# Attention and feed-forward in one kernel: scores of sequences 1 to 7 with queries on partitions, exponentials turned by DMA transposes

## The chip, the cores and the metric

The kernel runs on one core of one Trainium2 chip. The metric is the device time of one execution, in microseconds (us). The core has five engines, each with its own queue of instructions that it works off strictly in order: TensorE (PE; its weight loads are listed apart as PEld), VectorE (DVE), ScalarE (ACT), GpSimd (POOL) and SyncE (SP, which here issues all DMAs). They wait for one another through semaphores.

## The reference, cut to what matters

Eight sequences of 576 tokens, eight heads of 64. Causal softmax attention is mixed, by a gate per head, with a read from a memory matrix; the result goes through a two-layer feed-forward network (FFN).

```python
scores = q @ k.T / sqrt(64)                      # per sequence and head, 576 x 576
scores = where(causal, -1e9, scores)
a = exp(scores - scores.max(-1)); a /= a.sum(-1) + 1e-9
local = a @ v
mem_out = (phi(q) @ M_prev) / (phi(q) @ z_prev + 1e-6)
x = g * mem_out + (1 - g) * local                # 4608 tokens x 512
h = x @ w_in                                     # 512 -> 2048
out = (h * clip(h + 3, 0, 6) / 6) @ w_out        # 2048 -> 512
```

## The kernel before

**FFN.** 4608 tokens are 18 blocks of 256. A block has 8 pieces of the first product (`ffn1`, L510: 24 matmuls of 256 columns into a PSUM tile `ph`, of which there are two; then ACT, DVE, ACT and DVE at L531 to L534 make the two float16 parts of `g`) and 8 pieces of the second (`ffn2`, L536: 12 matmuls of 512 columns; after four pieces ACT moves the sum out at L554 and SP stores it). Float32 products are made of three float16 products, high by high, high by low and low by high. Block 0 and the whole of sequence 0 use float32 matmuls instead.

**Attention.** A unit is one head of one sequence with one group of 128-query blocks: blocks 0 and 1 together, block 2, block 3, block 4 (64 queries). With 8 heads that is 32 units a sequence. Of sequences 1 to 7 a unit goes through these steps:

- `scores` (L330): keys on partitions, queries along the row. For each tile of 128 keys two matmuls (L347, L348: high and low part of q) and, for the tile on the diagonal, a third one that adds the causal mask (L350).
- `reduce` (L352): the maximum over the key tiles on DVE (L360; block 0 is copied by ACT, L358), and then over partitions by POOL's `partition_all_reduce` (L362).
- `sub` (L364): DVE takes the maximum off (L368). `exp` (L375): ACT makes the exponentials (L377), and POOL writes them as float16, `ah`, with an `affine_select` whose condition always holds (L381).
- `lo` (L384): DVE makes the low part, `al` (L389).
- `pv` (L391): with `ah` and `al` as weights, three matmuls a key tile against v (L413 to L415), and two against the memory (L417).
- `combine` (L419): DVE and ACT divide, scale and add (L430 to L438).

**Preparation.** While a sequence is worked on, the four pairs of heads of the next are loaded and split into float16 parts (`prep_steps`, L162). Each pair has one `partition_all_reduce` on POOL (L186) for its scales, whose result DVE takes up at L190 and L143; each sequence's memory has one (L298), and each FFN block one for the scale of its x (L472). SP moves the halves of q, k and phi(q) into stacked tiles (L210, L211, L218) and turns x with `dma_start_transpose` (L496).

**Order.** The loop at L731 emits unit t's scores, unit t-1's exponentials and unit t-2's products, with FFN pieces between. `at` (L135) gives everything emitted a priority in pieces of the FFN; a scheduler then puts each engine's instructions into one fixed order. Five of the FFN's 18 blocks are left to the end (`TAIL`, L50).

Of the kernel before, what the change touches and what calls it, by code (L numbers as in the profile page):

```python
# [12 lines left out]
F32 = mybir.dt.float32  # L13
# [49 lines left out]
) + PREP_AT[2:]  # L63
LN_SA = float(np.log(SA))


@with_exitstack
def kernel(ctx, tc, qT, kT, v, mz, beta, w_in, w_out, out):
    nc = tc.nc
    PE, DVE, ACT, POOL, SP = nc.tensor, nc.vector, nc.scalar, nc.gpsimd, nc.sync  # L70
    B, NP, _, S = qT.shape          # 8, 4, 128, 576
    H = 2 * NP
    D = 64
    NT, DM = out.shape              # 4608, 512
# [41 lines left out]
    kst, qhl, qps, vst, raw, nat = [], [], [], [], [], []  # L116
    for i in range(NSLOT):
        sizes = [2 * NB * P, 4 * S, 2 * S, NB * 2 * 129]
        whole = const.tile([P, sum(sizes) + 2], F16, name=f"slot{i}")
        at = 0  # L120
        for lst, n, pat, kw in zip((kst, qhl, qps, vst), sizes,
                                   ["p (h s) -> p h s", "p (x h s) -> p x h s", "p (h s) -> p h s",
                                    "p (t h e) -> p t h e"],
                                   [dict(h=2), dict(x=2, h=2), dict(h=2), dict(t=NB, h=2)]):
            lst.append(whole[:, at:at + n].rearrange(pat, **kw))
            at += n
# [33 lines left out]
    slots = {}  # L160

    def prep_steps(b, p):  # L162
# [25 lines left out]
        def scale():  # L188
# [5 lines left out]
            DVE.scalar_tensor_tensor(scal[:, 0:1], i[:, 0:1], 0.125, i[:, 1:2], op0=ALU.mult, op1=ALU.mult)  # L194
            DVE.tensor_scalar(scal[:, 1:2], s[:, 0:1], s[:, 1:2], 8.0 * LN_SA, op0=ALU.mult, op1=ALU.mult)
# [5 lines left out]
            esc, shift = scal[:, 0:1], scal[:, 1:2]  # L201
            slots[b, p] = dict(sl=sl, esc=esc, shift=shift, coef=coef, eps=eps)
# [43 lines left out]
    def nat_load(p, part):  # L246
        """a pair of heads of sequence 0, for float32 products"""
# [65 lines left out]
    # a unit: some 128-query blocks of one head, their scores in one PSUM bank, keys on partitions  # L313
    UNITS = [(0, 1), (2,), (3,), (4,)]
    xtiles = {}
    groups = {}

    class Unit:
        def __init__(self, b, u, p, h):
            self.b, self.u, self.p, self.h = b, u, p, h  # L320
            self.blocks = []
            c = mcol = 0
            for i in UNITS[u]:
                self.blocks.append((i, rows[i], c, mcol))
                c += (i + 1) * rows[i]
# [483 lines left out]
```

## Time and profile before

| | |
|---|---|
| time, two runs | 1120.67 and 1122.51 us, median 1121.59 us |
| span of the profiled execution, first to last instruction | 1120.2 us |
| mean granted TensorE clock | 0.996 |
| HBM read, written | 48.14 MB, 9.44 MB |

The span of the profiled execution and the time of the runs differ by 1.4 us, so what lies outside the span is small. In the profile an engine's busy time is a sum over its instructions; matmuls are pipelined, so a matmul's own duration (0.27 us for 256 columns) is longer than the distance at which the next one starts (0.11 us). What a matmul costs is read from that distance. A group row gives the source line, the engine, the operation, what is written from what, the shape, the count, the busy sum, the mean of one, and the idle time of the engine in front of it with what ended that.

### The profile page before, as it was taken

The page shows a single profiled execution, that of the slowest core. Times are in us where ns is not written, and L with a number is a line of the kernel's source. Part 1 is how long each engine was busy: PE and PEld are TensorE (multiplying, and loading weights), DVE is VectorE, ACT ScalarE, POOL GpSimd, SP SyncE. Part 2 cuts the span into 40 slices and gives each one's busy share as a digit, 9 for nine tenths or more (in the row PEclk, how much of TensorE's full clock was granted, in tenths as well). Part 3 has the DMA queues.
Part 4 walks back from the last instruction along what each step waited for, and adds up shares of the span by engine and source line. Part 5 has one row for each costly group of instructions (what it writes and reads, how often), then busy time and mean ns, then how long its engine had stood idle before and what let it go on. Part 6 is the DMA issues. An engine that isn't in the chain of part 4 may idle for free.

```text
span 1120.2 us, 28768 instructions
## 1 busy us (share of the span) xinstructions
PE 1083.2 (97%) x10736; PEld 797.4 (71%) x10736; DVE 930.7 (83%) x2436; ACT 791.1 (71%) x1880; POOL 412.2 (37%) x544
## 2 busy tenths in 40 slices
PE   8999999999999899999999999999999999999998
PEld 6888767586767667676768576867685868685664
DVE  5999889899899969998999988888799968893321
ACT  5787879677877778787877787668686857563321
POOL 3322223444444433554244533354344433341000
PEclk9999999999999999999999999999999999999999
DMA  8734452333424343315332434233404230101100
GB/s 263 291 100 160 119 135 70 94 91 87 116 84 106 70 118 89 97 45 138 97 76 71 101 96 102 76 92 97 116 22 107 77 69 14 36 5 36 27 13 19
DMA packets 101468, 101.39 MB, mean 91 GB/s; under 512 B 50256, under 2 KB 80976, under 8 KB 101328
## 3 DMA queue, kind: packets, MB, share of 16 engines
q1 hardware_dynamic: 101328, 99.56, 33.1%
q8 instruction: 84, 1.38, 0.5%
q14 instruction: 56, 0.46, 0.1%
HBM read 48.14 MB, written 9.44 MB: 51 GB/s over the span
## 4 chain that ended last, share of the span: by engine, by line
PE 42%; DVE 32%; ACT 8%; issue 8%; DMA 6%; POOL 2%; SPq 1%; DVEq 0%; ACTq 0%; POOLq 0%
DVE a L368 6%; PE po L546 5%; PE po L548 5%; PE po L547 5%; PE ph L523 5%; DVE rm L360 5%; PE ph L524 4%; PE ph L525 4%; DVE al L389 4%; DVE r L532 3%; PE ph L518 3%; DVE g L534 2%; PE sT L343 2%; DVE W L157 2%; POOL mb L362 2%
## 5 line engine op out<-in xcount | busy, mean ns | idle before, releaser
L362 POOL PARTITION_ALL_REDUCE mb<-rm x256 | 251.7, 983 | 336.7 <-DVE rm L360 237.4
L523 PE MATMUL ph<-x,W 128*128 128x256 f16 x1088 | 297.6, 274 | 12.7 <-DVE r L532 7.3
L525 PE MATMUL ph<-x,W 128*128 128x256 f16 x1088 | 297.5, 273 | 0.0
L524 PE MATMUL ph<-x,W 128*128 128x256 f16 x1088 | 297.4, 273 | 0.0
L381 POOL TENSOR_SCALAR_AFFINE_SELECT ah<-a 128x384 f16<-128x384 f32 (+2 forms) x224 | 145.4, 650 | 214.4 <-ACT a L377 105.4
L546 PE MATMUL po<-W,g 128*128 128x512 f16 x544 | 206.6, 380 | 1.9 <-ACT ot L554 1.6
L548 PE MATMUL po<-W,g 128*128 128x512 f16 x544 | 206.5, 380 | 0.8 <-DVE g L534 0.8
L547 PE MATMUL po<-W,g 128*128 128x512 f16 x544 | 206.7, 380 | 0.0
L377 ACT ACTIVATE a<-a,scal 128x384 f32<-128x384 f32 (+2 forms) x224 | 141.6, 633 | 57.0 <-DVE a L368 48.8
L368 DVE SCALAR_TENSOR_TENSOR a<-sT,scal,mb 128x128 f32<-128x128 f32 (+4 forms) x280 | 147.2, 541 | 13.3 <-POOL mb L362 12.4
L360 DVE TENSOR_REDUCE rm<-sT 128x128 f32<-128x256 f32 (+3 forms) x256 | 135.6, 530 | 11.5 <-PE sT L350 4.6
L389 DVE TENSOR_TENSOR al<-a,ah 128x384 f16<-128x384 f32 (+2 forms) x224 | 134.0, 598 | 9.2 <-POOL ah L381 8.0
L532 DVE SCALAR_TENSOR_TENSOR r<-r,ph 128x512 f32<-128x512 f32 x136 | 92.1, 677 | 53.2 <-ACT r L531 52.6
L436 ACT ACTIVATE x<-o,cf 128x64 f32<-128x64 f32 (+1 forms) x320 | 100.6, 314 | 44.2 <-DVE cf L432 39.5
L531 ACT ACTIVATE r<-ph,bias_g,gsc 128x512 f32<-128x512 f32 x136 | 106.5, 783 | 34.2 <-PE ph L525 29.1
L347 PE MATMUL sT<-slot 128*128 128x128 f16 (+1 forms) x840 | 123.7, 210 | 3.9 <-DVE a L368 2.1
L348 PE MATMUL sT<-slot 128*128 128x128 f16 (+1 forms) x840 | 124.3, 210 | 0.0
L523 PEld LDWEIGHTS <-W 128*128 128x128 f16 x1088 | 106.8, 98 | 23.1 <-issue 6.6
L413 PE MATMUL o<-slot,ah 128*128 128x65 f16 (+1 forms) x840 | 116.3, 195 | 6.9 <-ACT y L437 3.6
L533 ACT ACTIVATE g<-r 128x512 f16<-128x512 f32 x136 | 86.4, 636 | 51.2 <-DVE r L532 51.1
L524 PEld LDWEIGHTS <-W 128*128 128x128 f16 x1088 | 106.7, 98 | 19.5 <-issue 5.0
L414 PE MATMUL o<-slot,ah 128*128 128x64 f16 (+1 forms) x840 | 115.4, 195 | 0.0
(149 smaller groups left out, 2387.4 us busy)
## 6 DMA issues: line engine op xcount, KB each, us to landing
slot<-q SPq DMA_DIRECT2D x112, 144.0 KB, 2.5
out<-ot SPq DMA_DIRECT2D x36, 256.0 KB, 2.0
stv<-vn SPq DMA_DIRECT2D x28, 320.0 KB, 3.3
W<-w_in SPq DMA_DIRECT2D x8, 1024.0 KB, 9.5
slot<-w_out SPq DMA_DIRECT2D x8, 1024.0 KB, 4.9
stq<-qT SPq DMA_DIRECT2D x28, 288.0 KB, 3.1
stk<-kT SPq DMA_DIRECT2D x28, 288.0 KB, 3.3
slot<-k SPq DMA_DIRECT2D x112, 72.0 KB, 2.0
```

Of the source, the lines that this page charges most:

```text
L360: DVE.tensor_reduce(rm[:, m0:m0 + nq], src.rearrange("p (t q) -> p q t", q=nq), axis=AX.X, op=ALU.max)
L362: POOL.partition_all_reduce(mb[:, 0:self.m], rm[:, 0:self.m], P, RMAX)
L368: DVE.scalar_tensor_tensor(a[:, c0:c0 + w].rearrange("p (t q) -> p t q", q=nq), self.sT[:, c0:c0 + w].rearrange("p (t q) -> p t q", q=nq), ...
L377: ACT.activation(a, a, AF.Exp, scale=slots[self.b, self.p]["esc"])
L381: POOL.affine_select(self.ah[:, 0:self.n], a, pattern=[[0, self.n]], compare_op=ALU.is_ge, fill=0.0, base=1, channel_multiplier=0)
L389: DVE.tensor_tensor(self.al[:, 0:n], self.a[:, 0:n], self.ah[:, 0:n], op=ALU.subtract)
L523: PE.matmul(ph[:, m], wh, f["xh"][:, c], start=c == 0, stop=False)
L524: PE.matmul(ph[:, m], wh, f["xl"][:, c], start=False, stop=False)
L525: PE.matmul(ph[:, m], wl, f["xh"][:, c], start=False, stop=c == 3)
L546: PE.matmul(po, gh[:, m, ts], W2[:, m, 0:512], start=m == 0, stop=False)
L547: PE.matmul(po, gh[:, m, ts], W2[:, m, 512:], start=False, stop=False)
L548: PE.matmul(po, gl[:, m, ts], W2[:, m, 0:512], start=False, stop=m == 15)
```

## The change

For sequences 1 to 7, and for these alone:

- **Scores** have queries on partitions and keys along the row: for each query block two matmuls (high and low part of k) of up to 512 columns. No mask matmul is left. Block 4 takes both heads of a pair at once, one in partitions 0 to 63 and the other in 64 to 127, in two PSUM tiles (512 and 64 columns), so it has one unit for two heads; a sequence has 28 units.
- **Reduce**: one DVE call (`tensor_tensor_reduce`) scales, adds the mask and keeps the minimum along the row (the scale is negative). POOL's all-reduce of the maximum, DVE's subtraction and ACT's copy are gone.
- **Exp**: ACT with the extremum as bias, one call per query block. POOL then writes the high float16 part with a `tensor_scalar` that multiplies by 256; before, that factor was in the exponent.
- **Lo**: DVE makes the low part. High and low stand side by side in one tile, and SP turns it with one `dma_start_transpose` into tiles with keys on partitions.
- **pv** reads the turned tiles; its matmuls are as many as before. It is emitted three units behind the scores instead of two (`PV_D`).
- q's and k's parts change places in the stacked tiles; a mask is built at the start; `HLB` goes from 3 buffers to 2. The preparation's and the FFN's all-reduces on POOL stay.

```diff
-HLB = 3
+HLB = 2
+AB, A16B, ATB = 2, 2, 2
+PV_D = 3
...
         def do_q():
-            t, hi, lo = pair_tiles("q")
+            _, hi, lo = pair_tiles("q")
             split(hi, lo, st["q"][:, :S], st["s"][:, 0:1])
+            stack(qst[sl], hi, lo)
+
+        def do_k():
+            t, hi, lo = pair_tiles("k")
+            split(hi, lo, st["k"][:, :S], st["s"][:, 1:2])
             for h in range(2):
                 for r in range(2):
-                    SP.dma_start(qhl[sl][D * r:D * r + D, :, h], t[D * h:D * h + D])
...
+                    SP.dma_start(khl[sl][D * r:D * r + D, :, h], t[D * h:D * h + D])
...
-                        kk = kst[sl][:, h, j * P:(j + 1) * P]
-                        PE.matmul(o, kk, qhl[sl][:, 0, h, q0:q0 + nq], start=True, stop=False)
-                        PE.matmul(o, kk, qhl[sl][:, 1, h, q0:q0 + nq], start=False, stop=j < i)
...
+            for i, nq, c0, _ in self.blocks:
+                for h in self.heads:
+                    r0 = D * h if self.both else 0
+                    w = min((i + 1) * P, S)
+                    for part in range(len(self.sT)):
+                        k0, k1 = 512 * part, min(512 * part + 512, w)
+                        o = self.sT[part][r0:r0 + nq, (c0 if part == 0 else 0):][:, 0:k1 - k0]
+                        for x in range(2):
+                            PE.matmul(o, qst[sl][:, h, i * P:i * P + nq], khl[sl][:, x, h, k0:k1],
+                                      start=x == 0, stop=x == 1)
...
+            a = self.a = p2.tile([P, S], F32, name=f"a_{self.id}", tag="a", bufs=AB)
+            nm = self.nm = small.tile([P, 2], F32, name=f"nm_{self.id}", tag="nm", bufs=6)
+            def masked(o, src, m, init, acc):
+                DVE.tensor_tensor_reduce(o, src, m, sd["nesc"], init, ALU.add, ALU.min, acc)
...
-            ACT.activation(a, a, AF.Exp, scale=slots[self.b, self.p]["esc"])
...
-            self.ah = p2.tile([P, 512], F16, name=f"ah_{self.id}", tag="ah")
-            POOL.affine_select(self.ah[:, 0:self.n], a, pattern=[[0, self.n]], compare_op=ALU.is_ge,
-                               fill=0.0, base=1, channel_multiplier=0)
...
+                ACT.activation(a, a, AF.Exp, bias=self.nm[:, c:c + 1], scale=-1.0)
...
+            POOL.tensor_scalar(self.hl[:, 0, 0:self.m], self.a[:, 0:self.m], SA, 1.0, op0=ALU.mult, op1=ALU.mult)
...
-            DVE.tensor_tensor(self.al[:, 0:n], self.a[:, 0:n], self.ah[:, 0:n], op=ALU.subtract)
...
+            DVE.scalar_tensor_tensor(self.hl[:, 1, 0:m], self.a[:, 0:m], SA, self.hl[:, 0, 0:m],
+                                     op0=ALU.mult, op1=ALU.subtract)
+            nb = 2 * self.n // P
+            self.aT = p2.tile([P, 2 * NB, P], F16, name=f"aT_{self.id}", tag="aT", bufs=ATB)
+            SP.dma_start_transpose(out=self.aT[:, 0:nb], in_=self.a16)
```

**What stands where.** On POOL, in the middle of sequence 5 before the change, the all-reduces of the units (`mb`) and the conversions (`ah`) alternate, and the all-reduce of a pair's preparation (`amr`) stands among them:

```order
L381 AFFINE_SELECT ah_2_1_1_9643<-a_2_1_1_9640 128x512
L362 ISA mb_2_2_0_9671<-rm_2_2_0_9670 128x128
L362 ISA mb_2_2_1_9743<-rm_2_2_1_9742 128x128
L381 AFFINE_SELECT ah_2_2_0_9716<-a_2_2_0_9713 128x512
L186 ISA amr_2_10001<-am_2_9994 128x3
L362 ISA mb_2_3_0_9821<-rm_2_3_0_9820 128x128
L381 AFFINE_SELECT ah_2_2_1_9793<-a_2_2_1_9790 128x512
```

and now, at the turn of sequence 3 to 4 (the conversion, L435, is a TENSOR_SCALAR; L190 is the pair's all-reduce, L299 that of the memory):

```order
L190 ISA
L190 ISA amr_3_7427<-am_3_7420 128x3
L435 ISA
L435 TENSOR_SCALAR a_3_3_2_1_7225<-a_3_2_1_7188 128x576
L435 TENSOR_SCALAR a_3_3_3_1_7360<-a_3_3_1_7322 128x576
L435 TENSOR_SCALAR a_4_0_0_0_7442<-a_0_0_0_7403 128x384
L299 ISA
L299 ISA ammr_7501<-amm_7500 128x2
L435 ISA
L435 TENSOR_SCALAR a_4_0_0_1_7509<-a_0_0_1_7449 128x384
```

The units' all-reduces have gone. Rows of L190, L299, L534 and L435 have come that name no tile: one stands in front of an all-reduce that follows a conversion, and one in front of a conversion that follows an all-reduce. Over the whole program there are 89 such rows, 88 of them from the first conversion on (44 of each kind). Before the change the program has one, at its start (L655).

On DVE, before the change, in the same place of sequence 5, what takes up the pair's all-reduce (L190, then L143) stands between the units' work and the FFN's (L532 makes the first half of `g`):

```order
L389 TENSOR_TENSOR al_2_2_0_9746<-a_2_2_0_9713,ah_2_2_0_9716 128x512
L360 TENSOR_REDUCE rm_2_3_0_9820<-sT_2_3_0_9795 128x128
L190 TENSOR_SCALAR amr_2_10001<-amr_2_10001 128x1
L532 SCALAR_TENSOR_TENSOR r_10_11161<-r_10_11161,ph_10_11136 128x512
L143 TENSOR_SCALAR i_2_10066<-amr_2_10001 128x4
L438 TENSOR_TENSOR x_3_9625<-x_3_9625,y_2_1_1_3_9752 128x128
L144 TENSOR_SCALAR i_2_10066<-i_2_10066 128x4
```

and now (L441 makes the low part from POOL's high part, L194 and L147 take up the all-reduce, L594 and L596 are the FFN's, L492 belongs to `combine`):

```order
L441 SCALAR_TENSOR_TENSOR a_5_2_2_0_10556<-a_2_2_0_10531,a_5_2_2_0_10556 128x512
L500 TENSOR_TENSOR x_3_10537<-x_3_10537,y_2_0_1_3_10542 128x128
L594 SCALAR_TENSOR_TENSOR r_10_12164<-r_10_12164,ph_10_12139 128x512
L194 TENSOR_SCALAR amr_2_10825<-amr_2_10825 128x1
L147 TENSOR_SCALAR i_2_10888<-amr_2_10825 128x4
L596 TENSOR_TENSOR g_97<-r_10_12164,g_97 128x512
L148 TENSOR_SCALAR i_2_10888<-i_2_10888 128x4
L492 TENSOR_TENSOR cf_2_1_1_3_10655<-o_2_1_0_3_10561,scal_1_8433 128x4
L594 SCALAR_TENSOR_TENSOR r_12_12256<-r_12_12256,ph_12_12231 128x512
```

The all-reduce is taken up at the same distance as before, and FFN instructions stand behind it as before: L441, then two rows, then L194, with the FFN's L596 and L594 behind.

On SP the turned exponentials stand among the loads, the stacked parts and the stores of the output (L617), here in sequence 4:

```order
L212 DMA slot_107<-qp_1_8669 64x576
L213 DMA slot_107<-qp_1_8669 64x576
L617 DMA out<-ot_1_9365 128x512
L445 DMA_TRANSPOSE aT_1_3_1_8385<-a_4_1_3_1_8365 128x6x128
L445 DMA_TRANSPOSE aT_2_0_0_8460<-a_4_2_0_0_8439 128x8x128
```

where before the change no unit had a row on SP at all. There are 196 rows of L445 beside the 46 transposes of x.

More of the change, by code (lines that the diff above doesn't have):

```diff
@@ L193, in scale @@
             scal = small.tile([P, 4], F32, name=f"scal_{b}_{p}", tag="scal", bufs=8)
-            DVE.scalar_tensor_tensor(scal[:, 0:1], i[:, 0:1], 0.125, i[:, 1:2], op0=ALU.mult, op1=ALU.mult)
-            DVE.tensor_scalar(scal[:, 1:2], s[:, 0:1], s[:, 1:2], 8.0 * LN_SA, op0=ALU.mult, op1=ALU.mult)
+            DVE.scalar_tensor_tensor(scal[:, 0:1], i[:, 0:1], -0.125, i[:, 1:2], op0=ALU.mult, op1=ALU.mult)
             DVE.memset(scal[:, 2:3], SA * 1e-9)
@@ L314 @@
     UNITS = [(0, 1), (2,), (3,), (4,)]
+    LAST = len(UNITS) - 1
     xtiles = {}
@@ L320, in __init__ @@
             self.b, self.u, self.p, self.h = b, u, p, h
+            self.both = b > 0 and u == LAST
+            self.idle = self.both and h == 0
+            self.heads = (0, 1) if self.both else (h,)
             self.blocks = []
@@ L349, in scores @@
+                    PE.matmul(o, t["k"][r, j * P:(j + 1) * P], t["q"][r, q0:q0 + nq],
+                              start=True, stop=j < i)
                     if j == i:
                         PE.matmul(o, ident16, negm[:, 0:nq], start=False, stop=True)
-        def reduce(self):
-            rm = p1.tile([P, 256], F32, name=f"rm_{self.id}", tag="rm")
-            mb = self.mb = p2.tile([P, 256], F32, name=f"mb_{self.id}", tag="mb")
+        def scores(self):
+            if self.idle:
+                return
+            if self.b == 0:
+                self.scores_t()
+                return
+            sl = slots[self.b, self.p]["sl"]
+            self.sT = [ps_s.tile([P, 512], F32, name=f"s_{self.id}", tag="sT")]
+            if self.both:
+                self.sT.append(ps_s.tile([P, 512], F32, name=f"s2_{self.id}", tag="sT"))
+            for i, nq, c0, _ in self.blocks:
[8 more added lines that the diff above has]
+                                      start=x == 0, stop=x == 1)
@@ new lines, in reduce @@
+        def reduce(self):
+            if self.idle:
+                return
+            if self.b == 0:
+                self.reduce_t()
+                return
+            a = self.a = p2.tile([P, S], F32, name=f"a_{self.id}", tag="a", bufs=AB)
+            nm = self.nm = small.tile([P, 2], F32, name=f"nm_{self.id}", tag="nm", bufs=6)
+            sd = slots[self.b, self.p]
+            def masked(o, src, m, init, acc):
+                DVE.tensor_tensor_reduce(o, src, m, sd["nesc"], init, ALU.add, ALU.min, acc)
+            if self.both:
+                masked(a[:, 0:512], self.sT[0], mask[:, 0:512], 3e38, nm[:, 0:1])
+                masked(a[:, 512:S], self.sT[1][:, 0:D], mask2, nm[:, 0:1], nm[:, 1:2])
+                return
+            for k, (i, nq, c0, _) in enumerate(self.blocks):
+                w = (i + 1) * P
+                masked(a[:, c0:c0 + w], self.sT[0][:, c0:c0 + w], mask[:, 512 - i * P:640], 3e38, nm[:, k:k + 1])
@@ L355, in reduce, with reduce_t @@
+        def reduce_t(self):
+            rmb = p2.tile([P, 2 * NB * P], F16, name=f"rmb_{self.id}", tag="a16", bufs=A16B).bitcast(F32)
+            rm = rmb[:, 0:256]
+            mb = self.mb = rmb[:, 256:512]
             for i, nq, c0, m0 in self.blocks:
@@ L364, in sub @@
         def sub(self):
-            a = self.a = p2.tile([P, 512], F32, name=f"a_{self.id}", tag="a")
+            if self.b > 0:
+                return
+            a = self.a = p2.tile([P, S], F32, name=f"a_{self.id}", tag="a", bufs=AB)
             for i, nq, c0, m0 in self.blocks:
@@ L375, in exp @@
         def exp(self):
-            a = self.a[:, 0:self.n]
-            ACT.activation(a, a, AF.Exp, scale=slots[self.b, self.p]["esc"])
+            if self.idle:
+                return
             if self.b == 0:
+                a = self.a[:, 0:self.n]
+                ACT.activation(a, a, AF.Exp, scale=slots[self.b, self.p]["esc"])
                 return
-            self.ah = p2.tile([P, 512], F16, name=f"ah_{self.id}", tag="ah")
-            POOL.affine_select(self.ah[:, 0:self.n], a, pattern=[[0, self.n]], compare_op=ALU.is_ge,
-                               fill=0.0, base=1, channel_multiplier=0)
+            for k, (i, nq, c0, _) in enumerate(self.blocks):
+                a = self.a[:, c0:c0 + min((i + 1) * P, S)]
+                c = 1 if self.both else k
+                ACT.activation(a, a, AF.Exp, bias=self.nm[:, c:c + 1], scale=-1.0)
+            n = self.n
+            self.a16 = p2.tile([P, 2 * NB * P], F16, name=f"a16_{self.id}", tag="a16", bufs=A16B)[:, 0:2 * n]
+            self.m = S if self.both else n
+            self.hl = self.a16.rearrange("p (x n) -> p x n", x=2)
+            if self.both:
+                POOL.memset(self.hl[:, :, S:], 0.0)
+            POOL.tensor_scalar(self.hl[:, 0, 0:self.m], self.a[:, 0:self.m], SA, 1.0, op0=ALU.mult, op1=ALU.mult)
         def lo(self):
-            if self.b == 0:
+            if self.b == 0 or self.idle:
                 return
-            self.al = p2.tile([P, 512], F16, name=f"al_{self.id}", tag="al")
-            n = self.n
-            DVE.tensor_tensor(self.al[:, 0:n], self.a[:, 0:n], self.ah[:, 0:n], op=ALU.subtract)
+            m = self.m
+            DVE.scalar_tensor_tensor(self.hl[:, 1, 0:m], self.a[:, 0:m], SA, self.hl[:, 0, 0:m],
[3 more added lines that the diff above has]
+            SP.dma_start_transpose(out=self.aT[:, 0:nb], in_=self.a16)
         def pv(self):
-            b, p, h = self.b, self.p, self.h
+            if self.idle:
+                return
+            b, p = self.b, self.p
             mt = mem[b]["t"]
             for i, nq, c0, _ in self.blocks:
-                if h == 0:
+                if self.heads[0] == 0:
                     if b == 0 and i in OF and i < 2:
@@ L661 @@
     DVE.tensor_copy(negm, negf)
+    POOL.memset(mask[:, 0:512], 0.0)
+    POOL.memset(negf, 0.0)
+    POOL.affine_select(negf, negf, pattern=[[-1, P]], compare_op=ALU.is_ge, fill=-3e38, base=0,
+                       channel_multiplier=1)
+    DVE.tensor_copy(mask[:, 512:], negf)
+    for r in range(2):
+        DVE.tensor_copy(mask2[D * r:D * r + D], negf[D * r:D * r + D, D * r:D * r + D])
     DVE.memset(bias_g, TG / 2.0)
@@ L729, in ffn_piece @@
         return True
-    for t in range(NU + 2):
+    for t in range(NU + 3):
         if t < NU:
@@ L754 @@
             units[t].scores()
-        if t >= 2:
-            at(due(t - 2))
-            units[t - 2].pv()
+        if t >= PV_D and t - PV_D < NU:
+            at(due(t - PV_D))
+            units[t - PV_D].pv()
         if t < NU:
@@ L767 @@
             units[t - 1].lo()
-        if t >= 2:
-            at(due(t - 2))
-            units[t - 2].combine()
+        if t >= PV_D and t - PV_D < NU:
+            at(due(t - PV_D))
+            units[t - PV_D].combine()
         if t >= X_T:
```

67 lines of the change are left out of this document (30 added, 37 removed).

## The prediction

> **What bounds the kernel now.** I read the page first, then the busy time by stage.
>
> ```profile
> span 1120.2 us, 28768 instructions
> PE 1083.2 (97%) x10736; PEld 797.4 (71%) x10736; DVE 930.7 (83%) x2436; ACT 791.1 (71%) x1880; POOL 412.2 (37%) x544
> PE 42%; DVE 32%; ACT 8%; issue 8%; DMA 6%; POOL 2%; SPq 1%; DVEq 0%; ACTq 0%; POOLq 0%
> ```
> ```profile
> 160.00:1016.00 856.00, 830.56 (x9276) 611.57 (x9275) 769.78 (x2050) 640.06 (x1556) 365.31 (x492) 1.00 0.32 82
> 1016.00:1120.20 104.20, 98.44 (x672) 63.24 (x670) 26.15 (x46) 30.76 (x51) 0.38 (x1) 0.99 0.07 21
> ```
>
> The columns of the second view are PE, PEld, DVE, ACT and POOL busy in that stretch, then granted clock and DMA share. Sequences 1 to 7 fill 160 to 1016 us. There PE is busy 831 of 856 us, DVE 770, POOL 365; the clock is full. PE is the bound, with DVE close behind: the chain that ended last runs through PE for 42% and DVE for 32%. PE's idle time of 25 us in this stage is all that faster neighbours can give back.
>
> **PE's work.** A matmul costs the distance to the next start. In the PE timeline:
>
> ```profile
> 239.82 0.22 PE L348 MATMUL sT<-slot 128*128 128x128 f16 x1
> 239.87 0.22 PE L347 MATMUL sT<-slot 128*128 128x128 f16 x1
> ...
> 499.92 0.27 PE L523 MATMUL ph<-x,W 128*128 128x256 f16 x1
> 500.03 0.27 PE L524 MATMUL ph<-x,W 128*128 128x256 f16 x1
> ...
> 501.34 0.38 PE L546 MATMUL po<-W,g 128*128 128x512 f16 x1
> 501.55 0.38 PE L547 MATMUL po<-W,g 128*128 128x512 f16 x1
> ...
> 504.02 0.19 PE L348 MATMUL sT<-slot 128*128 128x64 f16 x1
> 504.05 0.19 PE L347 MATMUL sT<-slot 128*128 128x64 f16 x1
> ```
> ```profile
> L348 PE MATMUL sT<-slot 128*128 128x128 f16 x560 | 95.2, 219 | 0.0
> L348 PE MATMUL sT<-slot 128*128 128x64 f16 x280 | 29.1, 193 | 0.0
> ```
>
> That is 56 ns for 128 columns (mean of neighbouring steps), 109 for 256, 216 for 512 and 29 for 64: columns count, weight loads are hidden. Per head (56 of them in sequences 1 to 7, from the counts 560 = 56 x 10 and 280 = 56 x 5) the scores were 20 + 4 matmuls of 128 columns and 10 + 1 of 64, mask included: 24 x 56 + 11 x 29 = 1.66 us. Now they are two each of 128, 256, 384 (162 ns, between) and 512, and per pair of heads four of 512 and four of 64 for block 4: 2 x (56 + 109 + 162 + 216) + 2 x (216 + 29) = 1.58 us. 35 matmuls become 12, but the columns stay, and 56 x 0.08 = **4.5 us** is all. `pv` keeps its matmuls.
>
> **DVE and ACT.**
>
> ```profile
> L360 DVE TENSOR_REDUCE rm<-sT 128x128 f32<-128x512 f32 x64 | 43.4, 678 | 0.1
> L360 DVE TENSOR_REDUCE rm<-sT 128x128 f32<-128x256 f32 (+3 forms) x256 | 135.6, 530 | 11.5 <-PE sT L350 4.6 <-ACT rm L358 4.0 <-POOL mb L362 2.2
> L368 DVE SCALAR_TENSOR_TENSOR a<-sT,scal,mb 128x512 f32<-128x512 f32 x56 | 41.5, 740 | 2.4 <-POOL mb L362 2.2
> L368 DVE SCALAR_TENSOR_TENSOR a<-sT,scal,mb x280: 333/539/752, 156.2 to 1010.6; 128x128 f32<-128x128 f32 x56, 128x384 f32<-128x384 f32 x28, 128x512 f32<-128x512 f32 x28, 128x320 f32<-128x320 f32 x28
> L389 DVE TENSOR_TENSOR al<-a,ah 128x512 f16<-128x512 f32 x56 | 39.1, 698 | 0.5 <-POOL ah L381 0.4
> L389 DVE TENSOR_TENSOR al<-a,ah 128x384 f16<-128x384 f32 (+2 forms) x224 | 134.0, 598 | 9.2 <-POOL ah L381 8.0
> L377 ACT ACTIVATE a<-a,scal 128x512 f32<-128x512 f32 x56 | 40.5, 724 | 15.3 <-DVE a L368 12.4 <-DVE cf L432 1.9 <-DVE cf L431 0.7
> ```
>
> At 512 elements reduce and subtract were 0.68 + 0.74 us; the fused call is not in the trace. It is between one such pass (0.74) and both (1.42), since the order shows it as two rows, the second 128x1; I take one pass plus 0.15. There are 280 such calls in place of 224 reduces and 280 subtractions, so DVE loses about 224 x 0.53 - 280 x 0.15 = 77 us of 770. ACT loses its copy and has a few more exponentials: within 25 us. Neither is the bound, so this buys part of the 25 us in which PE stood: between 0 and 25, I take **10 us**. An extremum that isn't one instruction after all would cost DVE those 77 us back, not the span more than 10.
>
> **The turn through SP.**
>
> ```profile
> L496 SPq DMA_TRANSPOSE x<-W x46: 1194/1264/2816, 147.1 to 1060.4; - x46
> x<-W SPq DMA_TRANSPOSE x46, 3.2
> out<-ot SPq DMA_DIRECT2D x36, 256.0 KB, 2.0
> SPq L555 <- ACT ot L554: 191.4, 25, 28.1
> ```
>
> A transpose of up to 128x1024 takes SP 1.26 us to issue and lands 3.2 us after that starts. 196 more hold SP for 247 us of 856, and DMAs are busy a third of the stage, so there is room. The chain of a unit of block 2 from scores to weights was 0.68 + 0.98 (all-reduce, below) + 0.74 + 0.72 + 0.78 + 0.70 = 4.6 us; it becomes 0.89 + 0.72 + 0.78 + 0.70 + 3.2 = 6.3. In the new PE order the rows between a unit's last score and its first product come, by the steps above, to a median of 12.2 us of PE work (10.1 before). That hides the turn: **0 us**. Without that cover it would be up to 196 x 1.7 = 333.
>
> **The rest.** The parts of q and k change places with as many DMAs. With two `hl` buffers in place of three, a split in the preparation waits for the copies of the one before last.
>
> ```profile
> slot<-q SPq DMA_DIRECT2D x112, 144.0 KB, 2.5
> ```
>
> They land after 2.5 us. The preparation runs most of a sequence ahead, 856 / 7 = 122 us, which hides that; with that lead gone it would be up to 28 x 3 x 2.5 = 210 us. The mask at the start is five short instructions. Together **0 us**.
>
> **POOL.** Here I expect the time to be decided.
>
> ```profile
> L362 POOL PARTITION_ALL_REDUCE mb<-rm x256 | 251.7, 983 | 336.7 <-DVE rm L360 237.4 <-DVE cf L430 28.6 <-DVE cf L432 16.8
> L381 POOL TENSOR_SCALAR_AFFINE_SELECT ah<-a 128x512 f16<-128x512 f32 x56 | 43.4, 775 | 31.7 <-ACT a L377 31.4
> L186 POOL PARTITION_ALL_REDUCE amr<-am x28 | 13.3, 474 | 34.8 <-ACT junk L152 31.3 <-PE ph L525 1.6 <-PE o L417 1.0
> L655 POOLq MODIFY_POOL_CONFIG  x2: 11/11/11, 1.1 to 1.1; - x2
> 0.83 0.20 POOL masks.py:197 MEMSET ident<- 128x128 f32 x1
> 1.18 0.38 POOL L655 PARTITION_ALL_REDUCE warm<-warm  x1
> ```
>
> 224 all-reduces of 0.98 us go, and 224 conversions become 196 at about the same price: POOL's work halves. But the order has 88 new rows without a tile, on both sides of every all-reduce that is left. [...] `affine_select` needed no exchange beside the all-reduce (the rows alternate without one); `tensor_scalar` does. In before the pair costs nothing visible: the all-reduce starts 0.15 us after the MEMSET ends. [...]
>
> What a true exchange costs, no row shows. Below: the 0.1 us of this row. Above: the longest load, a megabyte.
>
> ```profile
> W<-w_in SPq DMA_DIRECT2D x8, 1024.0 KB, 9.5
> slot<-vn SPq DMA_DIRECT2D x4, 192.0 KB, 6.4
> slot<-kT SPq DMA_DIRECT2D x4, 160.0 KB, 7.2
> ```
> ```profile
> L669 ACT ACT_TABLE_LOAD x1 | 1.3, 1283 | 0.8 <-PEq L800 0.8
> ```
>
> ACT's table takes 1.3 us. [...]
>
> Behind it stand: the next conversion on POOL; on DVE first L194, which takes up the all-reduce, two rows behind a unit's low part, with the FFN's L596 and L594 behind it; later the unit's L441, which waits for POOL's conversion. DVE is in order, so the FFN's results stop too. An all-reduce between two conversions blocks POOL for 2 x 6.8 + 0.47 = 14.1 us. Cover: PE can fill the two `ph` tiles, 2 x 24 x 0.109 = 5.2 us, and DVE has the rows between L194 and the next L441, some 3 us. That leaves about 6 us an episode: 14.1 - 8.1. There are 43 episodes with a conversion on both sides: 43 x 6 = **258 us**. The bounds: with no cover 43 x 14.1 = 606; if products alone waited, 34 (third rival); at 0.1 us an exchange nothing.
>
> **Sum.** 1120.2 - 4.5 - 10 + 0 + 258 = 1364; the span stands 1.4 us below the median of the runs, so the time is **1365 us**.
>
> **The rivals.**
> - *The exchange is as cheap as the trace's only row.* For it: 0.1 us is the only measurement here. Against it: that row may have had nothing to exchange. Then 1121.6 - 4.5 - 10 = 1107 us, not slower; it decides as long as an exchange stays under 3.8 us, where two of them and 0.47 are within the cover of 8.1.
> - *Cheap exchange, but the turn comes late on SP.* SP stood 191 us in 25 waits before stores of the output, 7.7 us each, up to 28; a transpose queued behind one waits along, and with `aT` in two buffers the next ones too. The PE order leaves a unit 12.2 - 6.3 = 5.9 us. If half of the 36 stores held up one unit by 7.7 - 5.9 = 1.8 us, it is 32 us; if each held up the two units behind it, 130: about 1107 + 80 = 1187. It decides once SP's delays pass those 5.9 us.
> - *Dear exchange, mostly covered.* From the last score of the unit before an episode to the first product of the unit behind it, the new PE order holds a median of 19.6 us of work by the same steps; the chain takes 6.3, which leaves 13.3 for 14.1. If only the products waited and DVE didn't hold up the FFN: 43 x 0.8 = 34 us, 1141. Against it: L194 and L441 stand in DVE's one queue.
>
> **Chances.** Forecast 0.72; cheap exchange 0.18; late turn 0.05; covered exchange 0.05. The range of the forecast alone, exchanges of 4.5 to 8.5 us (43 x (2 x 4.5 + 0.5 - 8.1) = 60, and 43 x 9.4 = 404), is 1166 to 1510. The two other slower rivals reach a little lower, and the range as a whole is **1140 to 1510**; the cheap exchange's 1107 is left out, with the 2 in 10 that go with it. A change of 2%, 22 us, is about what a measurement of this kernel can tell from none. Faster than 1099 comes only from the cheap exchange with more of PE's 25 us regained: 0.06. Within 2%: most of the rest of that case, and a sliver of the covered one: 0.13. Slower: 0.81.
>
> **What would show it.** In the profile after: 178 MODIFY_POOL_CONFIG; gaps of 5 us and more on POOL in front of each first conversion and first all-reduce; PE busy well under 85% in the stage of sequences 1 to 7; DVE waiting for POOL at L194 and L441 for some hundreds of us, where it waited 8 for the conversions in before. The score matmuls' busy sum falls, with little gained. If POOL starts a conversion within 0.2 us of the all-reduce's end while its input stands ready, the forecast is wrong. If PE's waits name DMA landings of `aT` with POOL long done, it was the turn.

## The result, and the profile after

The kernel after took 1441.9 us (two runs, 1441.03 and 1442.78) against 1121.59 before: a ratio of 1.286, 95% interval 1.282 to 1.289. It is 320 us slower; the forecast was 1365, with a range of 1140 to 1510. The profiled execution of it has a span of 1439.2 us.

The page's first lines and its chain:

```profile
span 1439.2 us, 26587 instructions
PE 1153.3 (80%) x9448; PEld 780.7 (54%) x9448; DVE 818.3 (57%) x2433; ACT 789.7 (55%) x1852; POOL 187.3 (13%) x323
PE 35%; issue 22%; DMA 16%; ACT 11%; DVE 11%; POOL 3%; SPq 2%; DVEq 0%; ACTq 0%; POOLq 0%
```

DVE and POOL have less work than before, 818 us for 931 and 187 for 412; ACT has the same. PE has 1288 matmuls fewer and is nevertheless busy for 70 us longer. In the chain that ended last "issue" now stands for 22%: that is time in which an engine waited for nothing the profile can name.

The stage of sequences 1 to 7 now runs to some 1340 us. The columns are PE, PEld, DVE, ACT and POOL busy, granted clock, DMA share and GB/s:

```profile
160.00:1340.00 1180.00, 904.35 (x8053) 599.24 (x8051) 662.88 (x2066) 644.01 (x1544) 143.64 (x270) 0.88 0.48 100
1340.00:1439.20 99.20, 93.32 (x617) 60.00 (x615) 25.38 (x42) 29.29 (x46) 0.39 (x1) 1.00 0.08 22
```

PE is busy for 904 of 1180 us, 77%, where it was 97%. No engine is a bound any more; they wait for one another. The granted clock is 0.88, which no step of the prediction had.

The waits, longest first, and below them POOL's MODIFY_POOL_CONFIG rows at two lines (count, then shortest, median and longest in ns, first and last start):

```profile
POOL a L435 <- ACT a L428: 268.1, 72, 12.5
DVE a L441 <- POOL a L435: 241.3, 98, 7.5
POOL a L435 <- issue: 185.7, 26, 7.8
POOL a L435 <- DMA aT<-a: 153.3, 54, 6.0
...
DVE amr L194 <- POOL amr L190: 84.4, 24, 5.8
...
POOL amr L190 <- issue: 77.6, 13, 6.3
...
DVE xm L536 <- POOL xr L534: 56.3, 16, 5.7
```
```profile
L435 POOLq MODIFY_POOL_CONFIG  x88: 82/83/85, 157.0 to 1286.9; - x88
L190 POOLq MODIFY_POOL_CONFIG  x44: 1/11/11, 178.1 to 1186.5; - x44
```

The row itself takes 11 to 83 ns (medians). They come in pairs: from the first conversion on 44 ahead of an all-reduce that follows other work on POOL and 44 ahead of the work that follows an all-reduce; "exchange" is the name of such a pair here. What one costs stands in the waits for "issue": 185.7 / 26 = 7.1 us ahead of a conversion, 77.6 / 13 = 6.0 us ahead of a pair's all-reduce. Where a wait for data ended later, the profile names that, and the exchange lies underneath: in POOL's timeline none of the 44 gaps ahead of an all-reduce is under 5.7 us, and none of the 44 ahead of the conversion that follows one is under 6.8. DVE, with its one queue, waits for POOL in three lines for 241.3 + 84.4 + 56.3 = 382 us.

One such episode in the timelines of POOL and of DVE (start, duration, engine, line, operation; in brackets the idle time in front of it):

```profile
600.84 0.38 POOL L190 PARTITION_ALL_REDUCE amr<-am  x1 [5.82 <-issue]
608.73 0.99 POOL L435 TENSOR_SCALAR a<-a 128x384 f16<-128x384 f32 x2 [7.51 <-ACT a L428]
```
```profile
597.46 0.67 DVE L594 SCALAR_TENSOR_TENSOR r<-r,ph 128x512 f32<-128x512 f32 x1
601.25 0.15 DVE L194 TENSOR_SCALAR amr<-amr 128x1 f32<-128x1 f32 x1 [3.12 <-POOL amr L190]
...
609.27 0.86 DVE L441 SCALAR_TENSOR_TENSOR a<-a,a 128x384 f16<-128x384 f32 x1 [2.00 <-POOL a L435]
```

From 595.0 (5.82 us ahead of the all-reduce) to 609.7 POOL does 1.4 us of work in 14.7 us. DVE stands twice, 3.1 us for the all-reduce and 2.0 us for the conversion; between the two it works off other rows. So DVE pays for the episode in two portions.

### The profile page after: what moved, and what is told of

Same layout as the page of the kernel before. It is cut to its first block, busy times and chain, and to the rows that moved or that the text cites. A ratio compares the mean times of both kernels' runs of the same rounds, so it can differ in the third digit from the quotient of the medians.

```text
span 1439.2 us, 26587 instructions
## 1 busy us (share of the span) xinstructions
PE 1153.3 (80%) x9448; PEld 780.7 (54%) x9448; DVE 818.3 (57%) x2433; ACT 789.7 (55%) x1852; POOL 187.3 (13%) x323
## 2 busy tenths in 40 slices
DMA packets 286933, 147.15 MB, mean 102 GB/s; under 512 B 235728, under 2 KB 266448, under 8 KB 286800
## 4 chain that ended last, share of the span: by engine, by line
PE 35%; issue 22%; DMA 16%; ACT 11%; DVE 11%; POOL 3%; SPq 2%; DVEq 0%; ACTq 0%; POOLq 0%
DMA aT<-a 10%; PE ph L585 4%; PE ph L587 4%; PE ph L586 4%; PE po L608 3%; PE po L610 3%; PE sT L345 3%; PE po L609 3%; DVE a L441 2%; POOL a L435 2%; PE ph L580 2%; PE s L368 2%; DMA slot<-k 2%; PE o L466 2%; DVE a L382 2%
## 5 line engine op out<-in xcount | busy, mean ns | idle before, releaser
L441 DVE SCALAR_TENSOR_TENSOR a<-a,a 128x384 f16<-128x384 f32 (+2 forms) x196 | 130.7, 668 | 241.6 <-POOL a L435 241.3
L428 ACT ACTIVATE a<-a,nm 128x128 f32<-128x128 f32 (+4 forms) x252 | 142.3, 584 | 165.5 <-DVE nm L382 98.9
L435 POOL TENSOR_SCALAR a<-a 128x384 f16<-128x384 f32 (+2 forms) x196 | 120.9, 619 | 697.8 <-ACT a L428 268.1
L368 PE MATMUL s<-slot 128*128 128x256 f16 (+5 forms) x672 | 128.6, 316 | 88.9 <-DVE nm L382 82.8
L475 PE MATMUL o<-slot,aT 128*128 128x65 f16 (+1 forms) x840 | 112.9, 203 | 101.8 <-DMA aT<-a 80.2
L475 PEld LDWEIGHTS <-aT 128*128 128x128 f16 (+1 forms) x840 | 85.2, 106 | 115.3 <-DMA aT<-a 96.7
L382 DVE CUSTOM_DVE_ANT_0 a<-s,mask,scal 128x128 f32<-128x128 f32 (+2 forms) x252 | 137.7, 565 | 17.2 <-PE s L368 15.3
L585 PEld LDWEIGHTS <-W 128*128 128x128 f16 x1088 | 112.7, 104 | 58.0 <-DVE r L594 29.3
L586 PEld LDWEIGHTS <-W 128*128 128x128 f16 x1088 | 112.6, 103 | 57.9 <-issue 37.0
L594 DVE SCALAR_TENSOR_TENSOR r<-r,ph 128x512 f32<-128x512 f32 x136 | 92.6, 681 | 57.7 <-ACT r L593 57.4
L587 PEld LDWEIGHTS <-W 128*128 128x128 f16 x1088 | 112.7, 104 | 22.6 <-issue 2.6
L368 PEld LDWEIGHTS <-slot 128*128 128x128 f16 (+1 forms) x672 | 53.8, 105 | 127.7 <-issue 102.6
L476 PE MATMUL o<-slot,aT 128*128 128x64 f16 (+1 forms) x840 | 112.4, 202 | 0.0
```

What stands on the lines that cost most here:

```text
L368: PE.matmul(o, qst[sl][:, h, i * P:i * P + nq], khl[sl][:, x, h, k0:k1], start=x == 0, stop=x == 1)
L382: DVE.tensor_tensor_reduce(o, src, m, sd["nesc"], init, ALU.add, ALU.min, acc)
L428: ACT.activation(a, a, AF.Exp, bias=self.nm[:, c:c + 1], scale=-1.0)
L435: POOL.tensor_scalar(self.hl[:, 0, 0:self.m], self.a[:, 0:self.m], SA, 1.0, op0=ALU.mult, op1=ALU.mult)
L441: DVE.scalar_tensor_tensor(self.hl[:, 1, 0:m], self.a[:, 0:m], SA, self.hl[:, 0, 0:m], op0=ALU.mult, op1=ALU.subtract)
L475: PE.matmul(o, ah, vv[:, j, h, 0:D + 1], start=j == 0, stop=False)
```

## The experiments

One thing holds for all of them: the scheduler plans the order of every engine anew for each kernel, so a difference of a few us between two kernels may be the order and not the edit. Each was timed beside the kernel before on the same chip (1119.0, 1120.1, 1121.0 and 1121.3 us); the intervals are of the ratio to it. The kernel after was timed beside 1121.6.

### The exchange taken away: e1_affine and e4_act

```diff
-            POOL.tensor_scalar(self.hl[:, 0, 0:self.m], self.a[:, 0:self.m], SA, 1.0, op0=ALU.mult, op1=ALU.mult)
+            POOL.affine_select(self.hl[:, 0, 0:self.m], self.a[:, 0:self.m], pattern=[[0, self.m]],
+                               compare_op=ALU.is_ge, fill=0.0, base=1, channel_multiplier=0)
```

> The changed kernel with one edit: POOL writes the high part with the always-true affine_select of before, without the factor 256 (so the low part and the small constant are without it as well). [...] If the exchanges cost the time (88 of them, 5.8 us before an all-reduce and 7.1 us before a conversion in the profile after), this runs at 1107 us, between 1090 and 1140, and PE's clock is back over 0.98. If the turn through SP and its buffers cost it, it stays above 1300 us.

Measured: 1154.8 us, ratio 1.030 (1.026 to 1.035). The only exchange left, the waits of DVE, and the page:

```profile
L718 POOLq MODIFY_POOL_CONFIG  x2: 12/12/12, 1.1 to 1.1; - x2
```
```profile
DVE a L442 <- POOL a L435: 88.6, 85, 3.6
...
DVE amr L194 <- POOL amr L190: 11.4, 15, 1.9
```
```profile
span 1156.3 us, 26399 instructions
PE 1081.9 (94%) x9448; PEld 749.4 (65%) x9448; DVE 818.0 (71%) x2433; ACT 787.1 (68%) x1852; POOL 194.5 (17%) x323
```

Another instruction for the conversion (the factor of 256 goes with it) brings back 287 us (1441.9 - 1154.8; 284 when each is taken against the kernel before that was timed beside it, 320 and 36 us), although POOL's busy time is even 7 us longer. DVE's waits for POOL in the same three lines fall from 382 to 111 us (the third is 10.7), by 271. PE's busy time falls by 71 us for the same 9448 matmuls. But the kernel is still 36 us slower than before, where 12 us faster was expected.

```diff
-            POOL.tensor_scalar(self.hl[:, 0, 0:self.m], self.a[:, 0:self.m], SA, 1.0, op0=ALU.mult, op1=ALU.mult)
+            ACT.activation(self.hl[:, 0, 0:self.m], self.a[:, 0:self.m], AF.Copy, scale=SA)
```

> The changed kernel with one edit: ACT writes the high part (a copy with scale 256) in place of POOL. No exchange is left either. If the exchanges cost the time, this runs near the kernel with affine_select: ACT gets 196 x 0.62 = 120 us on top of 790, which leaves it below PE; 1095 to 1150 us. If POOL's work between ACT and DVE is what delays the units, it is clearly faster than that kernel; if the turn decides, it stays above 1300 us.

Measured: 1151.3 us, ratio 1.028 (1.023 to 1.033), the same as e1_affine with another engine doing the conversion, and with the factor of 256 in place. So what e1_affine took away is the alternation on POOL and not the factor, and the 36 us that remain don't depend on who converts.

### The exchange put where it wasn't: e2_affine_exch and e3_before_exch

```diff
+            POOL.tensor_scalar(am[:, 2:3], am[:, 2:3], 1.0, 1.0, op0=ALU.mult, op1=ALU.mult)
             POOL.partition_all_reduce(amr[:, 0:3], am, P, RMAX)
```

Into e1_affine:

> The kernel without exchanges, plus one tensor_scalar of 128x1 (times 1) on POOL in front of each of the 28 all-reduces of a pair's preparation: 28 pairs of exchanges come back, and no conversion changes. If an exchange pair costs what it did in the changed kernel, 335 us for 43 pairs or 7.8 us each, this is 28 x 7.8 = 218 us above the kernel without exchanges, about 1325 us (1230 to 1400). If the exchanges are harmless, it stays within 2% of that kernel.

Into the kernel before:

> The kernel before the change, plus the same tensor_scalar of 128x1 in front of each pair's all-reduce: 28 pairs of exchanges in a kernel with none of the change. If an exchange is dear by itself, 28 pairs of 12.9 us with a third to two thirds of it covered add 28 x 4 to 28 x 9 = 112 to 252 us: 1235 to 1375 us, and the granted clock falls below 0.95. If the loss comes from the change's other parts, this stays within 2% of 1122 us.

Measured: 1456.4 us, ratio 1.300 (1.292 to 1.307), and 1435.8 us, ratio 1.281 (1.274 to 1.288). A single column multiplied by one, 28 times, makes the kernel before as slow as the change does. That is 301.6 / 28 = 10.8 and 316.8 / 28 = 11.3 us for two exchanges, more than either theory gave, and more than the change's own 287 / 43 = 6.7 us an episode. The waits of DVE in e2_affine_exch and the exchange's own time in it show what is different:

```profile
DVE amr L195 <- POOL amr L191: 297.5, 28, 13.0
...
POOL am L190 <- issue: 180.0, 25, 8.7
POOL amr L191 <- issue: 164.4, 28, 6.3
```

Here both exchanges lie in front of the same all-reduce, and DVE takes them as one stall of 10.6 us on average (297.5 / 28; 257.4 / 24 = 10.7 in e3_before_exch). In the change the first lies in front of the all-reduce and the second in front of a later conversion; DVE's stall at L194 is 84.4 / 24 = 3.5 us. A reading that fits the three numbers is that two short stalls are covered twice and one long stall once. It is not shown: no experiment moved the two exchanges apart and changed nothing else.

### Where the other 36 us are: more room for the turn, e5_buf3 and e6_later

In e1_affine PE and its weight loads stood 90 times (78 us) for landings of turned exponentials, so the first theory was the turn's lateness.

```diff
-AB, A16B, ATB = 2, 2, 2
+AB, A16B, ATB = 2, 2, 3
...
+            if self.both:
+                self.aX = []
+                for x in range(2):
+                    t = p2.tile([P, 8, P], F16, name=f"aT_{self.id}", tag="aT", bufs=ATB)
+                    SP.dma_start_transpose(out=t[:, 0:nb // 2], in_=self.a16[:, x * self.n:(x + 1) * self.n])
+                    self.aX.append(t)
+                return
```

> e1_affine with three buffers for the turned exponentials in place of two. To make room each buffer holds 8 blocks of 128 in place of 10, and the turn of block 4 goes in two transposes, each to a buffer of its own (28 transposes more). e1_affine took 1154.8 us, 36 more than before, and its products waited 78 us, 90 times, for landings of aT. If the buffers make the turn late (SP waits for products to give back a buffer, then the transpose takes 3.2 us more): 1135 to 1145. If the chain from scores to landing is simply longer than PE's other work at those places: 1150 to 1157, as in e1_affine. If the 36 us have nothing to do with the turn: 1155.

```diff
+        late = [t - d for d in (4, 3) if 0 <= t - d < NU and (units[t - d].b > 0) == (d == 4)]
+        for w in late:
+            at(due(w))
+            units[w].pv()
```

> e5_buf3 with the products of sequences 1 to 7 one unit later: four units behind the scores in place of three, about 4.4 us of PE work more between a unit's scores and its products (856 us over 196 units). If the lateness of the turn, from whatever cause, is what PE stands for: 1120 to 1130, and the waits for aT nearly gone. If the 36 us have nothing to do with the turn: 1150 to 1160.

Measured: 1167.3 us, ratio 1.042 (1.038 to 1.046), and 1176.1 us, ratio 1.050 (1.047 to 1.053). Both are slower than e1_affine, which no theory had. Both also issue 28 transposes more, since the turn of block 4 goes in two, so they don't test the third buffer alone. In e6_later the products still wait, and the conversions wait more, for landings:

```profile
POOL a L435 <- DMA aT<-a: 250.5, 98, 10.1
...
PEld L484 <- DMA aT<-a: 52.2, 48, 3.3
```

In e1_affine these two waits were 227.7 us (83 times) and 46.5 (50). A unit more between scores and products doesn't bring the landings ahead of the products. This speaks against a landing that is late by a fixed amount.

### The turn without those who wait for it: e7_noturn to e11_copy

The next five separate the transposes from the waits for them. In e7_noturn the products read a constant tile:

```diff
-                        ah = self.aT[:, c0 // P + j, r0:r0 + nq]
-                        al = self.aT[:, (self.n + c0) // P + j, r0:r0 + nq]
+                        ah = aC[:, r0:r0 + nq]
+                        al = aC[:, r0:r0 + nq]
```

> e1_affine with products that take their weights from a constant tile of 128x128 and no longer from the turned exponentials; the exponentials, their conversion and all transposes are still issued, with the same buffers, but no product waits for them. It leaves out the use of the softmax weights, so its output is not the attention. If PE's wait for landings makes the 36 us: 1120 to 1130. If the transposes cost through the load that they put on SP and the DMA engines: 1150, little change. If the fused extremum or the wide score matmuls are slower than their rows say: 1150 too.

And e8_nodma issues no transposes besides:

```diff
-            self.aT = p2.tile([P, 2 * NB, P], F16, name=f"aT_{self.id}", tag="aT", bufs=ATB)
-            SP.dma_start_transpose(out=self.aT[:, 0:nb], in_=self.a16)
```

> e7_noturn without the 196 transposes themselves. It leaves out the use of the softmax weights and their turn. Against e7_noturn it shows what the transposes cost by occupying SP (247 us of issue) and the DMA engines (share 0.64 against 0.32 in before): by the wait theory the same as e7_noturn within 5 us; by the load theory 1120 to 1130 where e7_noturn stays at 1150.

Measured: 1148.1 us, ratio 1.026 (1.021 to 1.030), and 1112.6 us, ratio 0.994 (0.991 to 0.997). The wait of the products is worth at most some 7 us: the intervals of e1_affine and e7_noturn overlap. The 196 transposes cost 35.5 us with no product waiting for them. Without them the kernel is 7.5 us faster than before. That is an upper bound, give or take the new order, for what the change's other parts are worth together: the products of e8_nodma wait for no exponentials at all, and in before PE stood 4.4 us for them (at L413 for `ah`, at L415 for `al`). What PE waits for, first in e7_noturn, then in e8_nodma (busy sum and mean, then the idle time in front):

```profile
L587 PE MATMUL ph<-x,W 128*128 128x256 f16 x1088 | 300.5, 276 | 29.9 <-DMA x<-W 15.0 <-DVE r L596 14.6
```
```profile
L585 PE MATMUL ph<-x,W 128*128 128x256 f16 x1088 | 298.4, 274 | 13.8 <-DMA x<-W 8.4 <-DVE r L594 4.5 <-DVE i_x L149 0.6
```

PE's wait has moved from the products to the FFN: 16 us more there, 7 for the turn of x on the same queue and 10 for DVE. DVE stands behind POOL, first in e7_noturn, then in e8_nodma:

```profile
DVE a L443 <- POOL a L436: 94.7, 92, 3.0
```
```profile
DVE a L443 <- POOL a L436: 41.0, 52, 2.2
```

And POOL stands, in e7_noturn alone, behind the transposes, which must land before a conversion may write over its buffer:

```profile
POOL a L436 <- DMA aT<-a: 107.2, 46, 5.2
...
POOL a L435 <- DMA aT<-a: 56.4, 18, 6.4
```

So there were two theories left, this buffer and the load that a transpose is for SP and the DMA engines. Three kernels on the base of e7_noturn try them. The transposes read a constant, so that no other engine waits for them and they wait for none:

```diff
-            SP.dma_start_transpose(out=self.aT[:, 0:nb], in_=self.a16)
+            SP.dma_start_transpose(out=self.aT[:, 0:nb], in_=W1[:, 0:2].rearrange("p a b -> p (a b)")[:, 0:2 * self.n])
```

> e7_noturn (1148.1 us) with transposes that read a constant part of W1 in place of the converted exponentials: the same 196 transposes of the same sizes on SP's queue, but no conversion waits for them to give back its buffer, and SP doesn't wait for DVE's low parts ahead of them. It leaves out the turn and the use of the softmax weights. e8_nodma, without transposes, took 1112.6. If what costs is that the conversions wait for the transposes (in e7_noturn POOL waited 107 + 56 us for their landings, in e8_nodma not at all): 1110 to 1120. If it is the load on SP and the DMA engines: 1140 to 1150.

A third buffer for the converted exponentials:

```diff
-AB, A16B, ATB = 2, 2, 2
+AB, A16B, ATB = 2, 3, 2
...
-            n = self.n
-            self.a16 = p2.tile([P, 2 * NB * P], F16, name=f"a16_{self.id}", tag="a16", bufs=A16B)[:, 0:2 * n]
+            n = self.n = min(self.n, 512)
+            self.a16 = p2.tile([P, 8 * P], F16, name=f"a16_{self.id}", tag="a16", bufs=A16B)[:, 0:2 * n]
```

> e7_noturn with three buffers for the converted exponentials in place of two; to make room the unit of block 4 converts and turns 512 of its 576 keys. It leaves out the use of the softmax weights, and those 64 keys. If the two buffers are the cost: POOL's wait for landings nearly gone and 1115 to 1128. If the load of the transposes is: 1143 to 1150.

A plain copy in place of the transpose:

```diff
-            SP.dma_start_transpose(out=self.aT[:, 0:nb], in_=self.a16)
+            SP.dma_start(self.aT[:, 0:nb], self.a16.rearrange("p (c t) -> p c t", t=P))
```

> e7_noturn with a plain DMA copy of the same bytes in place of each transpose: the same waits on SP and the same buffers held until a landing, but issue and landing as a plain DMA (some 0.6 and 2 us in place of 1.24 and 3.2). It leaves out the turn and the use of the softmax weights. If the waits behind a DMA are the cost, in proportion to its length: about 1148 - 35 x (1 - 2.0/3.2), 1130 to 1138. If it is what a transpose does to SP and the DMA engines: 1112 to 1120.

Measured: e9_load 1187.8 us, ratio 1.060 (1.056 to 1.065); e10_a16 1136.9, ratio 1.015 (1.012 to 1.019); e11_copy 1116.8, ratio 0.995 (0.993 to 0.997).

The buffer is a part of it. In e10_a16 POOL's largest wait is for ACT, its input, and the one for landings is small:

```profile
POOL a L434 <- ACT a L429: 541.9, 163, 16.0
...
POOL a L434 <- DMA aT<-a: 13.5, 6, 4.4
```

That is worth up to 1148.1 - 1136.9 = 11 us; a small part of it may be the 64 keys of block 4 that this kernel neither converts nor turns (192 blocks of 128 a sequence in place of 200). Another 24 remain against e8_nodma, with nobody waiting for a landing to speak of. In e9_load no engine but SP waits for a landing of `aT` (SP 47 us, for a buffer to turn into), and the time is 75 us above e8_nodma: the transposes alone, as a load, can cost more than the 35 us. It doesn't give the size of that cost in the change, since these transposes, which wait for no low part, were issued closer together: from 88.7 to 664.7 us, where those of e7_noturn ran from 169.0 to 1047.4.

The copy is the sharpest of the three. It has the same bytes, waits on SP for the same low parts, and holds the same buffers until a landing; POOL even waits 113 us for it. The row of the issuing line, first in e7_noturn, then in e11_copy (shortest, median and longest time of the issue on SP, in ns), and the time to landing:

```profile
L447 SPq DMA_TRANSPOSE aT<-a x196: 1209/1238/2562, 169.0 to 1047.4; - x196
...
DMA to landing us min/median/max: 2.7/3.1/5.8
```
```profile
L447 SPq DMA_DIRECT2D aT<-a x196: 464/478/1671, 167.3 to 1009.4; - x196
...
DMA to landing us min/median/max: 2.1/2.3/5.5
```

It holds SP for 0.48 us in place of 1.24 and lands after 2.3 in place of 3.1, and the 35.5 us shrink to some 4. At these sizes, 128x768 to 128x1280 elements of two bytes, a transpose is dearer than the copy of the same bytes by 2.6 times on the issuing queue, by a third in the landing, and by 31 us in the kernel's time.

The page's rows on DMA queues, the same two kernels in the same order (packets, MB, share of 16 engines):

```profile
q1 hardware_dynamic: 286800, 145.46, 57.5%
```
```profile
q1 hardware_dynamic: 129552, 145.44, 45.5%
```

Nearly the same bytes, in more than twice the packets.

### SP's queue: e12_act_queue

```diff
-                SP.dma_start(dst[0:D, h, :S], hi[D * h:D * h + D])
+                ACT.dma_start(dst[0:D, h, :S], hi[D * h:D * h + D])
...
-            SP.dma_start(out[n * TB + t * P:n * TB + (t + 1) * P, :], o)
+            ACT.dma_start(out[n * TB + t * P:n * TB + (t + 1) * P, :], o)
```

> e1_affine (1154.8 us) with 148 plain DMAs moved from SP's queue to ACT's, where ACT has just made their data: the 36 stores of the output and the 112 copies of the high parts of q and of the positive map of q into the slots. SP then holds all 242 transposes and what is left of the loads. If a transpose costs because it holds SP for 1.24 us (a plain copy of the same bytes: 0.48 us and only 4 us of span in all) and later issues stand behind it, freeing SP of 148 issues and of its waits for the output brings back a part: 1135 to 1148. If SP's queue has no part in it, the issues cost ACT time only: 1153 to 1165.

Measured: 1161.7 us, ratio 1.037 (1.033 to 1.040): nothing came back. So either it isn't the time for which SP is held, or ACT's issues ate what SP's gave; the one kernel doesn't tell which. How the last 24 us divide among SP's issue, the DMA engines' packets and the longer landing stays open. That the transpose itself makes them, and a copy doesn't, is shown, for kernels whose products don't wait for the turn.

## Why the prediction was right, and where it was not

The terms as the runs give them: without transposes and exchanges -7.5 (e8_nodma); the transposes and the waits for exponentials +43.3 (from there to e1_affine's +35.8), both against the kernel before that was timed beside them; the exchanges +287.1 (1441.9 - 1154.8, not timed beside each other). From 1119.0 that makes 1441.9. The prediction's terms were -14.5, 0 and +258, from 1121.6. It is 77 us short: 43 by the turn, 29 by the exchanges, 7 by the smaller gain, less 2.6 by the other start.

- **The bound.** PE was the bound, and relief for DVE and POOL bought little: right. The gain without turn and exchange is at most 7.5 us of the 14.5 forecast. PE's busy time in e1_affine, 1081.9 us, is 1.3 below that of before, where the columns were to save 4.5; the granted clock there was 0.984 in place of 0.996.
- **The fused extremum.** At 512 elements it is two rows of 0.744 and 0.081 us, together 0.83, where 0.89 was taken. DVE's whole saving, 112 us, is larger than the 77 forecast; POOL's work halved, and ACT's didn't change, as said.

```profile
L382 DVE CUSTOM_DVE_ANT_0 a<-s,mask,scal 128x512 f32<-128x512 f32 x84 | 62.4, 744 | 9.0 <-PE s L368 8.1
...
L382 DVE DVE_READ_ACCUMULATOR2_ANT nm<- 128x1 f32 x280 | 22.6, 81 | 0.0
```

- **The exchange is real, and dear.** Shown from both sides, by e1_affine and e4_act, which take it away, and by e3_before_exch, which puts it into the kernel before. The 0.1 us in the trace of before tells nothing of this price: the same exchange at 1.1 us stands in e1_affine. Why that one costs next to nothing, no run shows. The price in the sum was 6.8 us each, the author's estimate from two DMA loads (192 KB in 6.4 us, 160 KB in 7.2); no run shows this term. The waits give 6.0 and 7.1, so an episode blocks POOL for 13.5 us with its all-reduce, where 14.1 was forecast. That it came out so near is luck as far as these runs go: no run shows a load behind an exchange. The kernel after moved 147.15 MB in 286933 packets, and e1_affine, without its 88 exchanges, 147.15 MB in 286932. What POOL does in these 6 to 7 us stays open. They are paid at every alternation in the kernel after and not only once: none of the 88 gaps is under 5.7 us.
- **The cover** was forecast at 8.1 us an episode, which left 6.0. The runs give 287.1 / 43 = 6.7. The stall goes through DVE's one queue, as said: DVE's waits for POOL fell by 271 us when the exchanges went. But part of it has another form than forecast. 71 of the 287 us are PE's longer busy time at a lower granted clock, which had no term; the rest, 216 / 43 = 5.0 us an episode, is standing still. And the cover is no constant: in e2_affine_exch two exchanges of 7.2 + 5.9 us cost 10.8. So the nearness of 258 to 287 is in part luck. The three rivals that priced the exchange as cheap or covered are out.
- **The turn at 0 us** is the step that failed. Its working looked at the chain of one unit, 6.3 us against 12.2 us of PE's other work, and found it covered. That was nearly true of the products (7 us by e7_noturn). It left out that a transpose is also a load that costs by itself (35.5 us, of which a copy costs some 4), and that a conversion has to wait until the turn of two units earlier has landed (up to 11 us). The rival with a late turn came nearer, but in another place: it blamed the 36 stores of the output on SP's queue, and e12_act_queue moved those away without a gain, though ACT's issues may have eaten one.
- **The rival of the cheap exchange** was given 1107 us and "not slower". With no exchange at all the change is 3% slower (e1_affine). The chance of it as a case that isn't slower was therefore too high, whatever the exchange had cost.
- **What would show it**: 178 rows of MODIFY_POOL_CONFIG were listed; 88 and 44 of them stand above, the other 46 at lines 299, 534 and 717. The gaps, PE's 77% and DVE's waits at L194 and L441 are all there. The sign of a late turn is there too: PE waited 80.2 us in 35 cases at L475 for landings of `aT`. In e1_affine that wait is 31.9 us, so most of it came with the exchanges.

## What to carry to other kernels

On POOL, count the exchanges (pairs of MODIFY_POOL_CONFIG rows), not only the instructions: a one-column multiplication ahead of an all-reduce, with two of them, cost 11 us here, and an instruction that does the conversion without an exchange (e1_affine), or another engine (e4_act), took the cost of the exchanges away. A DMA transpose is not a free turn because its latency is covered: 196 of them with no product waiting cost 35.5 us here. Look at its issue, its packets and the buffer that it holds until it lands, and compare with a plain copy in its place. When an in-order engine stands between two others, ask how many separate stalls it takes and how long each is: here two exchanges in one stall cost 11 us and in two stalls 7, though why isn't shown.

## What the runs showed of the hardware

- In the kernel after, the granted TensorE clock fell around stalls of PE, and the matmuls in such a stretch ran slower. PE stands from 638.8 to 645.2 us; the granted clock is 0.50 from 640.6 to 650.9, and a matmul of 256 columns then costs 0.21 us, behind it 0.11:

```profile
645.18 1.07 PE L368 MATMUL s<-slot 128*64 128x512 f16 x4 [6.41 <-DVE nm L382]
...
650.34 0.42 PE L586 MATMUL ph<-x,W 128*128 128x256 f16 x1
650.56 0.42 PE L587 MATMUL ph<-x,W 128*128 128x256 f16 x1
...
651.15 0.27 PE L585 MATMUL ph<-x,W 128*128 128x256 f16 x1
651.26 0.27 PE L586 MATMUL ph<-x,W 128*128 128x256 f16 x1
```

  There are 44 such stretches, 295 us together, where e1_affine has 8 with 39 us. In the 4 us ahead of one PE was busy for 28% on average, and over 61% only ahead of the last, at the end of the span. Two windows of 60 us (columns as above):

```profile
170.00:230.00 60.00, 32.14 (x292) 24.39 (x293) 29.54 (x94) 31.17 (x80) 4.93 (x11) 0.76 0.40 88
290.00:350.00 60.00, 45.52 (x491) 32.30 (x489) 33.49 (x106) 33.89 (x77) 8.00 (x15) 0.89 0.48 108
```

  Over the whole run the clock was 0.898, against 0.996 before, 0.984 in e1_affine and 0.894 in e3_before_exch. So part of what the stalls cost here is slower work: PE's 9448 matmuls were busy for 1153.3 us in the kernel after and for 1081.9 in e1_affine, 71 us more.
- POOL's `affine_select` and `partition_all_reduce` alternated with no exchange (e1_affine, before); `tensor_scalar` and `partition_all_reduce` didn't (the kernel after), in either direction, and the way back to `tensor_scalar` was the longer one (7.1 us against 6.0).
